# Counting longer landing times, and later TensorE requests, in the emission clock of a two-layer attention and SwiGLU kernel

## The chip, the cores and the metric

The kernel runs on one core of one Trainium2 chip. The metric is the device time of one execution in microseconds (us). Every device time quoted is a median of repeated runs. A profile shows one execution (before's is a further one, of 1567.82 us), and its span is 1 to 2 us shorter than its device time. TensorE is called PE, VectorE DVE, ScalarE ACT, GpSimd POOL, SyncE SP. "L656" is line 656 of the kernel.

## The reference

Two layers, each an attention block A and a SwiGLU block B with residuals, over 2048 tokens of width 1024 (abridged).

```python
def _A_ref(x, wqkv, wo):            # H = 32 heads of 32; W, dil = 8, 2
    qkv = ((x @ wqkv).reshape(B, S, 3, H, Dh)).transpose(2, 0, 3, 1, 4)
    q, k, v = qkv[0], qkv[1], qkv[2]
    idx = arange(S)[:, None] - (arange(W) * dil)[None, :]
    # gathered kg, vg: for each token its own and seven earlier tokens, two apart
    logits = einsum("bhsd,bhswd->bhsw", q, kg) * Dh ** -0.5      # -1e9 where idx < 0
    o = einsum("bhsw,bhswd->bhsd", softmax(logits), vg)
    return o.transpose(0, 2, 1, 3).reshape(B, S, D) @ wo

def _B_ref(x, w1, w3, w2):          # F = 3584
    return (silu(x @ w1) * (x @ w3)) @ w2

x = A_x
x = x + _A_ref(_layernorm(x), A_wqkv, A_wo)
x = x + _B_ref(_layernorm(x), B_w1, B_w3, B_w2)
x = x + _A_ref(_layernorm(x), A_wqkv, A_wo)        # the same weights again
x = x + _B_ref(_layernorm(x), B_w1, B_w3, B_w2)
```

## The kernel before

PE does the projections. The eight-neighbour attention has no matmul in its inner part: DVE multiplies q with shifted k (L582), folds the products (L502, L506), PE adds up heads with a 0/1 matrix (the "gather", L595), a softmax follows (DVE L616 to L628, ACT L620), POOL spreads the result over the partitions by four DMAs into `At` (L635), DVE multiplies `At` with shifted v and folds again (L656), and PE multiplies the result `oT` with wo (L762). One such round covers 256 tokens and is called a half here; there are 16.

Three stages follow each other. Stage A is layer 0's projections, up to the first gate matmul of B. The middle stage is the first two chunks of B (pg L1243, pu L1252, acc L1274). During it ACT and DVE also prepare scaled sums and differences of w1, w3 and w2 and store them to HBM. In the last stage the other six chunks of B use those stored sums with fewer matmuls (st L1122, w L1057). The rest of the attention is woven in everywhere.

All engines' instruction streams are written in an order that an *emission clock* decides while the program is built. `now["pe"]`, `now["dve"]`, `now["act"]` advance by counted costs. Background work is emitted when the clock says that it can run before the next thing which must be on time. At run time the engines take their streams in order and wait where data is missing, as the traces show it: in before DVE stood 5.96 us at one product with later instructions behind it, and PE 4.85 us at one matmul.

The parts of the kernel that matter here, cut where `...` stands:

```python
def background(until):                 # DVE work that fits before `until`
    while True:
        best = None
        for queue in (norms, makes, adds, values, scores):
            step = head(queue)
            if step is not None:
                start = max(now["dve"] + 0.3, step[1])
                if start - 0.3 + step[0] <= until and (best is None or start < best[0]):
                    best = start, queue
        if best is None:
            return
        take(best[1])

def pe_requests(limit=1, must=False):  # small matmuls that DVE or ACT asked PE for
    act_background()
    while pe_queue and limit and (must or pe_queue[0][0]() + 2.5 <= now["pe"]):
        pe_queue.pop(0)[1]()
        limit -= 1

def score_steps():                     # ... q, k products, gather, softmax, then
        At = Ats[l, h] = wk.tile([P, 4, W, BLK], BF16, name="At")
        for a in range(4):
            heads = An[32 * a:32 * (a + 1)]...
            nc.gpsimd.dma_start(At[:, a]..., heads)          # L635
        At_at[l, h] = now["dve"] + 6.0

def value_steps():
        ...
        yield 0.0, max(ready, At_at[l, h]), lambda: None     # not before At has landed
        yield from tree(KT, tree_bufs[1], mul_v, ...)        # L656: At * v

def weight_size(m, g, w, at, got):     # ACT sums squares of w1/w3, PE adds them up (L872)
        ...
        t = now["act"] + 0.3
        pe_queue.append((lambda: t, lambda: add_up(t)))      # the scaled copies wait for it
```

Of the kernel before, what the change touches and what calls it, by code (L numbers as in the profile page):

```python
# [17 lines left out]
def kernel(  # L18
# [67 lines left out]
    now = dict(pe=23.6, dve=15.0, act=24.5, table=None, sp=12.0, dma=31.5)  # L86
# [268 lines left out]
    def act_background():  # L355
        for queue in (acts, sizes, parts, reads):
            while True:
                s = head(queue)
                if s is None or max(now["act"], s[1]) + s[0] > now["pe"] + 2.2:
                    break  # L360
                take_act(queue)
# [180 lines left out]
    def load_qk(l, h):  # L542
        if (l, h) in qks or (l, h // R, 1) not in qkv_at:
            return
        qT = qkvp.tile([P, KT, TCH], BF16, name="qT")
        kT = qkvp.tile([P, KT, HALO + TCH], BF16, name="kT")
        load_part(qT, l, 0, h * TCH, False)
        qks[l, h] = qT, kT, load_part(kT, l, 1, h * TCH, True)
# [7 lines left out]
    pe_queue = []  # L556
    L_at, At_at, Ats, av_done = {}, {}, {}, set()
# [3 lines left out]
    def pe_requests(limit=1, must=False):  # L561

        act_background()
        while pe_queue and limit and (must or pe_queue[0][0]() + 2.5 <= now["pe"]):
            pe_queue.pop(0)[1]()
            limit -= 1

    def score_steps():

        V = nc.vector  # L570
        for g, (l, h) in enumerate(halves):
            load_qk(l, h)
            while (l, h) not in qks:
                yield "blocked"
                load_qk(l, h)
            load_v(l, h)
            qT, kT, ready = qks[l, h]
            psm = wk.tile([P, W, 2, TCH], BF16, name="psm")

            def mul_qk(w_, pr):  # L580
                k0 = HALO - DIL * w_
                V.tensor_tensor(pr, qT[:], kT[:, :, k0:k0 + TCH], op=ALU.mult)  # L582

            yield 0.0, ready, lambda: None
            yield from tree(W, tree_bufs[0], mul_qk, lambda w_: psm[:, w_], True)
            load_v(l, h)
            if g + 1 < len(halves):
                load_qk(*halves[g + 1])
            at = {}

            def gather_heads(t):
                at["L"] = L = side.tile([P, W, BLK], FP32, name="L", tag="sd")
                for i in range(2):
                    for a in range(4):
                        nc.tensor.matmul(L[32 * a:32 * (a + 1), :, :], lhsT=gather[:],  # L595
                                         rhs=psm[:, :, i, a * BLK:(a + 1) * BLK], start=i == 0, stop=i == 1,
                                         skip_group_check=True)
                at["t"] = pe(3, t) + 0.2

            while g and halves[g - 1] not in At_at:  # L600
                yield "blocked"
            t = now["dve"] + 0.2
            pe_queue.append((lambda: t, lambda: gather_heads(t)))
            while "t" not in at:
                yield "blocked"
            L = at["L"]
            mx = smp.tile([P, BLK], FP32, name="mx")
            E = smp.tile([P, W, BLK], BF16, name="E")
            sm_ = smp.tile([P, BLK], FP32, name="sm_")
            rs = smp.tile([P, BLK], FP32, name="rs")  # L610
            An = E
            yield 0.0, at["t"], lambda: None
            if h == 0:
                yield 0.2, 0.0, lambda: V.tensor_tensor(L[0:32, :, 0:HALO], L[0:32, :, 0:HALO], maskT[:],
                                                        op=ALU.add)
            yield 0.68, 0.0, lambda: V.tensor_reduce(mx[:], L[:].rearrange("p w e -> p e w"), op=ALU.max, axis=AX.X)  # L616

            def exps():
                V.tensor_tensor(L[:], L[:], mx[:].unsqueeze(1).to_broadcast([P, W, BLK]), op=ALU.subtract)
                nc.scalar.activation(E[:], L[:], ACTF.Exp, scale=scale)  # L620
                at["E"] = act(0.65, now["dve"] + 0.1, "exp")

            yield 0.70, 0.0, exps
            yield 0.0, at["E"] if "E" in at else 0.0, lambda: None
            yield 0.66, at["E"], lambda: V.tensor_reduce(sm_[:], E[:].rearrange("p w e -> p e w"), op=ALU.add,
                                                         axis=AX.X)
            yield 0.56, 0.0, lambda: V.reciprocal(rs[:], sm_[:])
            yield 0.68, 0.0, lambda: V.tensor_tensor(An[:], E[:], rs[:].unsqueeze(1).to_broadcast([P, W, BLK]),  # L628
                                                     op=ALU.mult)
            while g >= 1 and halves[g - 1] not in av_done:  # L630
                yield "blocked"
            At = Ats[l, h] = wk.tile([P, 4, W, BLK], BF16, name="At")
            for a in range(4):
                heads = An[32 * a:32 * (a + 1)].rearrange("h w e -> h (w e)").unsqueeze(1).to_broadcast([32, 4, W * BLK])
                nc.gpsimd.dma_start(At[:, a].rearrange("p w e -> p (w e)"), heads)  # L635
            At_at[l, h] = now["dve"] + 6.0

    def value_steps():

        V = nc.vector  # L640
        for g, (l, h) in enumerate(halves):
            while (l, h) not in At_at or (g >= 2 and o_todo.get(halves[g - 2], 1)):
                yield "blocked"
            load_v(l, h)
            while (l, h) not in vs:
                yield "blocked"
                load_v(l, h)
            At = Ats[l, h]
            vT, ready = vs[l, h]
            oT = wk.tile([P, KT, TCH], BF16, name="oT", bufs=2)  # L650
            oTs[l, h] = oT

            def mul_v(t, tm):
                base = vT[:, t, HALO:HALO + TCH]
                win = bass.AP(vT.tensor, base.offset, [list(base.ap[0]), [-DIL, W], [BLK, 4], [1, BLK]])
                V.tensor_tensor(tm.rearrange("p w (a e) -> p w a e", a=4), At[:].rearrange("p a w e -> p w a e"), win, op=ALU.mult)  # L656

            yield 0.0, max(ready, At_at[l, h]), lambda: None
            yield from tree(KT, tree_bufs[1], mul_v, lambda t: oT[:, t, :], False)
            oT_at[l, h] = now["dve"]  # L660
            o_todo[l, h] = 2
            av_done.add((l, h))
            if g + 1 < len(halves):
                load_v(*halves[g + 1])
# [189 lines left out]
    def weight_size(m, g, w, at, got):  # L854

        w_ = w[:].rearrange("p k c -> p (k c)")
        half = w_.shape[1] // 2
        up, down = up_scale[:, m, g:g + 1], down_scale[:, m, g:g + 1]
        for i in range(2):
            yield 1.95, at, lambda: nc.scalar.activation(junk, w_[:, i * half:(i + 1) * half], ACTF.Square,  # L860
                                                         accum_out=size[:, m, g, i:i + 1])

        def scale_item(ps, r):
            def emit():
                scale_of(ps[:], up, down)
                got["at"] = now["dve"] + 0.1
            yield 0.8, r, emit

        def add_up(t):
            ps = side.tile([P, 1], FP32, name="size", tag="sd")  # L870
            for i in range(2):
                nc.tensor.matmul(ps[:], lhsT=ones[:], rhs=size[:, m, g, i:i + 1], start=i == 0, stop=i == 1)  # L872
            makes.append([scale_item(ps, pe(2, t)), None])

        t = now["act"] + 0.3
        pe_queue.append((lambda: t, lambda: add_up(t)))

    def weight_sums(m, g, w, got):
# [78 lines left out]
    def scales2():  # L957

        def scale_item(ps, r):
            def emit():  # L960
                nc.vector.tensor_reduce(total[:], ps[:], op=ALU.add, axis=AX.X)
                scale_of(total[:], up2[:], down2[:])
                got2["at"] = now["dve"] + 0.1
            yield 1.1, r, emit

        def add_up(t):
            ps = side.tile([P, 16], FP32, name="size", tag="sd")
            nc.tensor.matmul(ps[:], lhsT=ones[:], rhs=size2[:], start=True, stop=True)
            makes.append([scale_item(ps, pe(1, t)), None])

        t = now["act"] + 0.3
        pe_queue.append((lambda: t, lambda: add_up(t)))

    got2 = {}
# [401 lines left out]
```

## Time and profile before

| | before |
|---|---|
| median of 3 runs (range) | 1570.33 us (1569.12 to 1570.57) |
| span of the profiled execution | 1566.1 us |
| PE stream at its own pace (below) | about 1519 us |
| PE waits, sum | 30.2 us |
| idle of DVE before value products L656 | 41.8 us |

The PE stream's own pace is a sum over its 9694 matmuls with the spacing that the trace shows when nothing is waited for (0.216 us between 128x512 matmuls, 0.109 between 128x256 ones). These are the head and two lines of the first part of the profile page:

```profile
span 1566.1 us, 25184 instructions
...
PE 1531.8 (98%) x9694; PEld 993.9 (63%) x9694; DVE 1193.6 (76%) x2048; ACT 881.6 (56%) x1386; POOL 155.0 (10%) x308
```

PE is busy 98% of the span, so only its gaps can be won. The next list, the waits of PE, says what each gap waited for: the waiting instruction and its line, what ended the wait, then total us, times, longest.

```profile
PE st L1122 <- DVE st L1163: 5.3, 2, 4.8
PE w L1057 <- DVE hsum L1028: 4.2, 3, 1.8
PE L L595 <- DVE psm L506: 3.9, 2, 2.7
PE w L1057 <- DVE hT L1028: 3.0, 4, 1.5
PE size L968 <- ACT hsum L937: 2.6, 1, 2.6
PE st L1122 <- ACT big L1160: 2.0, 1, 2.0
PE po L762 <- DVE x_sb L767: 1.7, 1, 1.7
PE w L1057 <- ACT big L1077: 1.7, 4, 0.6
PE pu L1252 <- DMA w3t<-in_B_w_dram: 1.4, 1, 1.4
PE st L1122 <- DVE big L1175: 1.4, 1, 1.4
PE po L762 <- DVE oT L506: 1.3, 2, 1.1
```

Left out are two start-up waits, 1.8 us together. No entry is larger than 5.3 us. Seven of the eleven, 20.8 of 28.5 us, name DVE, which is itself busy only 76% of the time, so DVE is not too slow but late at certain places. Its own waits show one that is plainly a scheduling matter:

```profile
DVE st L1163 <- ACT big L1160: 48.5, 27, 3.6
DVE tree L656 <- DMA At<-E: 38.1, 12, 7.3
...
DVE tree L656 <- DMA late<-t_d: 3.6, 1, 3.6
```

The value products wait 38.1 us for `At` in 12 of 16 halves (the 41.8 us of the table are these and the 3.6 us of the last line). How that reaches PE shows in the timeline around 860 us (start, duration, instruction, and in brackets the idle time before it with what ended it), first DVE, then PE:

```profile
852.00 1.55 DVE L1042 SCALAR_TENSOR_TENSOR x_sb<-w,down,x_sb 128x512 bf16<-128x512 f32 x2
859.51 1.23 DVE L656 TENSOR_TENSOR tree<-At,vT 128x2048 bf16<-128x2048 bf16 x1 [5.96 <-DMA At<-E]
...
862.98 0.69 DVE L1163 TENSOR_TENSOR st<-st,big 128x512 f32<-128x512 f32 x1
```

```profile
857.84 1.04 PE L1122 MATMUL st<-big,early 128*128 128x256 f16 x8
863.72 1.82 PE L1122 MATMUL st<-big,late 128*128 128x256 f16 x8 [4.85 <-DVE st L1163]
```

DVE stood 5.96 us at its value product. The addition L1163 that PE needed for its next block stood four instructions behind (at 862.98; the lines between are products and folds of the same half), and DVE did not pass over the waiting product in those 5.96 us. PE idled 4.85 us. The eight 128x256 matmuls that follow also took 1.82 us together instead of the usual 1.03 or so; the section on the result comes back to that.

### The profile page before, as it was taken

What the parts mean: (1) busy time and instruction counts of PE and PEld (TensorE: products, weight loads), DVE (VectorE), ACT (ScalarE), POOL (GpSimd) and SP (SyncE); (2) the same over time, 40 slices, a digit from 0 to 9 for tenths busy, and PEclk for the clock granted to TensorE, in tenths of its full rate; (3) what the DMA queues carried; (4) which work ended last, traced back from release to release, by engine and by line L of the source; (5) the groups of instructions that cost most, each with busy time, mean ns of one, the idle gap of its engine ahead of it and who ended that gap; (6) DMA issues with size and microseconds to landing.
All of it is one profiled execution on the core that took longest, in us unless ns stands there. A gap on an engine that the chain in (4) does not pass through costs nothing.

```text
span 1566.1 us, 25184 instructions
## 1 busy us (share of the span) xinstructions
PE 1531.8 (98%) x9694; PEld 993.9 (63%) x9694; DVE 1193.6 (76%) x2048; ACT 881.6 (56%) x1386; POOL 155.0 (10%) x308
## 2 busy tenths in 40 slices
PE   9999989999999999899999999999999999999999
PEld 7666634444444578575675757866677657676866
DVE  4789797888978879989796968897577977445345
ACT  3785366576566346555465554655648346544634
POOL 1210101111121100101011010100102000000000
PEclk9999999999999999999999999999999999999999
DMA  9676959699788898979979888897979977878885
GB/s 323 188 215 220 220 167 348 237 324 313 226 286 312 276 335 292 303 246 307 308 257 296 288 283 271 298 327 263 319 270 298 337 274 270 313 272 320 324 293 208
DMA packets 261432, 439.57 MB, mean 281 GB/s; under 512 B 73856, under 2 KB 201088, under 8 KB 245056
## 3 DMA queue, kind: packets, MB, share of 16 engines
q1 hardware_dynamic: 248464, 390.90, 75.2%
q0 software_dynamic: 12704, 46.93, 8.3%
q8 instruction: 76, 1.25, 0.3%
q14 instruction: 44, 0.36, 0.1%
q10 hardware_dynamic: 144, 0.13, 0.0%
HBM read 345.90 MB, written 67.90 MB: 264 GB/s over the span
## 4 chain that ended last, share of the span: by engine, by line
PE 77%; DVE 12%; DMA 7%; ACT 2%; issue 1%; POOL 1%; SPq 0%; DVEq 0%; ACTq 0%
PE st L1122 29%; PE ps L820 13%; PE w L1057 11%; PE po L762 6%; PE acc L1274 6%; PE pu L1252 5%; PE pg L1243 5%; DMA At<-E 3%; DVE tree L656 2%; DVE tree L502 2%; DVE tree L582 1%; DMA x_sb<-in_A_x_dram 1%; DMA w3t<-in_B_w_dram 1%; DVE hT L1028 1%; POOL At L635 1%
## 5 line engine op out<-in xcount | busy, mean ns | idle before, releaser
L820 PE MATMUL ps<-xnT,wqkv 128*128 128x512 f16 (+1 forms) x1472 | 320.7, 379 | 0.0
L1122 PEld LDWEIGHTS <-early 128*128 128x128 f16 x2688 | 263.3, 98 | 38.5 <-issue 1.0
L820 PEld LDWEIGHTS <-wqkv 128*128 128x128 bf16 x1472 | 210.7, 144 | 108.5 <-issue 2.5
L1057 PE MATMUL w<-t,hT 128*128 128x512 f16 x1008 | 226.5, 379 | 4.8 <-DVE hT L1028 3.0
L1122 PEld LDWEIGHTS <-late 128*128 128x128 f16 x2016 | 197.3, 98 | 40.1 <-issue 11.9
L656 DVE TENSOR_TENSOR tree<-At,vT 128x2048 bf16<-128x2048 bf16 x128 | 156.2, 1220 | 43.2 <-DMA At<-E 38.1
L1122 PE MATMUL st<-xnT,late 128*128 128x256 f16 x1344 | 174.3, 273 | 3.5 <-ACT big L1160 2.0
L582 DVE TENSOR_TENSOR tree<-qT,kT 128x2048 bf16<-128x2048 bf16 x128 | 156.3, 1221 | 26.5 <-DMA qT<-qkv_d 15.8
L502 DVE TENSOR_TENSOR tree<-tree 128x1024 bf16<-128x1024 bf16 x256 | 175.1, 684 | 0.9
L1057 PEld LDWEIGHTS <-hT 128*128 128x128 f16 x1008 | 98.0, 98 | 118.8 <-DVE hT L1028 5.8
L1122 PE MATMUL st<-big,early 128*128 128x256 f16 x1344 | 173.1, 273 | 0.3
L1122 PE MATMUL st<-xnT,early 128*128 128x256 f16 x1344 | 165.7, 273 | 0.0
L1151 ACT COPY st<-st 128x512 f32<-128x512 f32 x84 | 48.4, 576 | 127.3 <-PE st L1122 126.5
L762 PE MATMUL po<-wo,oT 128*128 128x512 bf16 x512 | 116.2, 379 | 3.0 <-DVE x_sb L767 1.7
L1252 PE MATMUL pu<-xnT,w3t 128*128 128x512 f16 x448 | 105.8, 379 | 1.4 <-DMA w3t<-in_B_w_dram 1.4
L1243 PE MATMUL pg<-xnT,w1t 128*128 128x512 f16 x448 | 107.1, 382 | 0.0
L824 ACT CAST hT<-ps 128x512 bf16<-128x512 f32 x96 | 55.7, 585 | 81.9 <-PE ps L820 78.4
L1274 PE MATMUL acc<-w2t,hT 128*128 128x512 bf16 x448 | 98.2, 379 | 0.0
L1163 DVE TENSOR_TENSOR st<-st,big 128x512 f32<-128x512 f32 x84 | 58.4, 695 | 48.7 <-ACT big L1160 48.5
L1131 ACT ACTIVATE sg<-st,down_scale 128x512 bf16<-128x512 f32 x126 | 86.4, 686 | 12.3 <-PE st L1122 11.8
L1122 PE MATMUL st<-big,late 128*128 128x256 f16 x672 | 87.9, 274 | 5.3 <-DVE st L1163 5.3
L762 PEld LDWEIGHTS <-oT 128*128 128x128 bf16 x512 | 50.0, 98 | 59.3 <-DVE oT L506 2.1
(166 smaller groups left out, 1905.9 us busy)
## 6 DMA issues: line engine op xcount, KB each, us to landing
early<-t_d SPq DMA_DIRECT2D x84, 1024.0 KB, 6.7
late<-t_d SPq DMA_DIRECT2D x84, 768.0 KB, 6.3
t<-t_d SPq DMA_DIRECT2D x42, 1024.0 KB, 6.8
t<-t_d SPq DMA_DIRECT2D x42, 768.0 KB, 5.3
wqkv<-in_A_wqkv_dram SPq DMA_DIRECT2D x28, 1024.0 KB, 8.5
w1t<-in_B_w_dram SPq DMA_DIRECT2D x14, 1024.0 KB, 8.4
w3t<-in_B_w_dram SPq DMA_DIRECT2D x14, 1024.0 KB, 11.8
t_d<-big POOLq DMA_DIRECT2D x28, 512.0 KB, 6.6
```

What stands on the lines that cost most here:

```text
L502: nc.vector.tensor_tensor(b, b, buf[:, 4:8, :], op=ALU.add)
L582: V.tensor_tensor(pr, qT[:], kT[:, :, k0:k0 + TCH], op=ALU.mult)
L656: V.tensor_tensor(tm.rearrange("p w (a e) -> p w a e", a=4), At[:].rearrange("p a w e -> p w a e"), win, op=ALU.mult)
L762: nc.tensor.matmul(ps[:], lhsT=oT[:, t, j * P:(j + 1) * P], rhs=wo[:, t, hh * 512:(hh + 1) * 512], start=(t == 0), stop=(t == KT - 1))
L820: nc.tensor.matmul(ps[:], lhsT=ws[kk // KH][:, kk % KH, t::KT], rhs=xnT[:, kk, :], start=(kk == 0), stop=(kk == KT - 1))
L1057: nc.tensor.matmul(out[:], lhsT=lhs[:, k, j * P:(j + 1) * P], rhs=w[:, k, :], start=start and k == 0, stop=k == nq - 1, skip_group_check=True)
L1122: nc.tensor.matmul(out[:, a, :], lhsT=w[:, a, blk, k, :], rhs=rhs[:, k, :], start=start and a == 0 and k == 0, stop=k == KQ - 1, skip_grou ...
L1131: nc.scalar.activation(sg[:], src, ACTF.Silu, scale=inv)
L1163: nc.vector.tensor_tensor(G["D"][:], G["D"][:], su, op=ALU.add)
L1243: nc.tensor.matmul(pg[:], lhsT=w1t[:, kk, fi * P:(fi + 1) * P], rhs=xnT[:, kk, :], start=(kk == 0), stop=(kk == KT - 1))
L1252: nc.tensor.matmul(pu[:], lhsT=w3t[:, kk, fi * P:(fi + 1) * P], rhs=xnT[:, kk, :], start=(kk == 0), stop=(kk == KT - 1))
L1274: nc.tensor.matmul(acc[:], lhsT=hT[:, f, j * P:(j + 1) * P], rhs=tiles[hh][f // nq][:, f % nq, :], start=(f == 0), stop=(f == f1 - f0 - 1))
```

## The change

The intent is that the emission clock should believe in longer latencies: `At` lands 11 us after its issue and not 6; q, k, v loads land 2 us later; small matmuls asked from PE stand 1 us later in its stream, and those for weight scales 2.2 us more. No arithmetic is added or removed. In before the 64 `At` pieces of 128 KB took 2.7 to 12.0 us from issue to landing, median 6.3; from the end of the product L628 to the last of a half's four landings it was 5.1 to 13.3 us.

```diff
@@ pe_requests
-        while pe_queue and limit and (must or pe_queue[0][0]() + 2.5 <= now["pe"]):
+        while pe_queue and limit and (must or pe_queue[0][0]() + 3.5 <= now["pe"]):
@@ score_steps
-            yield 0.0, ready, lambda: None
+            yield 0.0, ready + 2.0, lambda: None
...
-            At_at[l, h] = now["dve"] + 6.0
+            At_at[l, h] = now["dve"] + 11.0
@@ value_steps
-            yield 0.0, max(ready, At_at[l, h]), lambda: None
+            yield 0.0, max(ready + 2.0, At_at[l, h]), lambda: None
@@ weight_size, and the same line in scales2 (w2)
-        t = now["act"] + 0.3
+        t = now["act"] + 2.5
```

More of the change, by code (lines that the diff above doesn't have):

```diff
@@ L969, in add_up @@
             makes.append([scale_item(ps, pe(1, t)), None])
-        t = now["act"] + 0.3
+        t = now["act"] + 2.5
         pe_queue.append((lambda: t, lambda: add_up(t)))
```

## The prediction

> **What bounds it now.** TensorE. The page gives PE 98% busy (1531.8 of 1566.1 us), VectorE 76%, ScalarE 56%, clock 0.998. A 128x512 matmul issues every 0.216 us: about 1519 us for the PE stream. The waits of PE add up to only 30 us: st on VectorE's L1163 5.3, w on hsum 4.2 and on hT 3.0, the gather L on psm 3.9, size (L968) on hsum 2.6, st on ACT L1160 2.0, po on x_sb 1.7 and on oT 1.3, w on ACT L1077 1.7, pu on the w3t load 1.4, st on L1175 1.4, start-up 1.8. So about 28 us (1.8%) is the ceiling of what a reordering can give.
>
> **What the change does.** It adds and removes no arithmetic. The clock only decides where instructions stand in each in-order stream. [...]DVE waited 5.96 us for At before its tree at 859.5, the addition L1163 behind it came late, and PE sat 4.85 us.
>
> 1. At counted 11 us after its issue instead of 6. From the end of the E product (L628) to the last At piece's landing takes 5.1 to 13.3 us, median 8.8: 6 was nearly always too short. VectorE waited 38.1 us for At in 12 of 16 halves. In the new order the VectorE work between that product and the first value product, summed with measured durations, grows from typically 6 to 8 us to 11 to 12 (up to 18; one half keeps none). The waits for At should fall from 38 to under 12 us.
> 2. q, k and v counted 2 us later: small; the 15.8 us wait for the first qT is a start-up matter and stays.
> 3. PE requests 1 us later, weight-scale requests 2.2 us more: the first two gathers (stalls 2.7 and 1.2) and the size matmul (2.6) stand 16 matmuls, 3.4 us, later. Those 6.5 us should go. The fifth o tile, stalled 2.7 us around 207 to 220, stands 14 us later.
>
> ACT gets two more table loads, 1.28 us each.
>
> **Sum.** Late requests: -6. PE stalls behind At waits (L1163, hsum, hT, L1175, L1160, po: 18.6 us in all): perhaps two thirds, -12. New collisions in the reshuffled stream: +3. Net -15 us: 1555 us, range 1547 to 1564. Faster by over 2% needs 31 us, more than all stalls: 0.02. Slower by 2%: 0.01.
>
> **What the profile would show if right.** VectorE's waits for At under 12 us; waits of PE near 15 us in total, with the gather and the size matmul gone from the list; the 4.85 us stall near 860 gone; PE and VectorE busy times equal (1532, 1194 us). If At waits fall but PE waits stay near 30, new collisions ate the gain; if At waits stay, landing times grew, because DMAs moved too.
>
> **What would make it wrong.** Delayed value trees delay oT, the o tiles, the norm and its transposes: if one of those becomes what PE waits for at the start of a B stage, some us are lost each time (no such wait is there today). A softmax pushed onto a spot where ScalarE must switch tables just before the gate's silu (as near 626) can stall PE 2 to 5 us. Shifted loads can collide: late weights, like the w3t near 475, would show as PE waiting for a DMA.

On table loads, the traces show 27 in before and 29 in after, 1.28 us each, and near 626 us in before a PE wait of 2.01 us behind two of them; the 5 us of "2 to 5 us" is not shown.

## The result

| | before | after |
|---|---|---|
| median (range), 4 runs each | 1569.72 us (1565.77 to 1570.57) | 1546.71 us (1546.08 to 1548.26) |
| profiled span | 1566.1 us | 1546.5 us |
| PE waits, sum | 30.2 us | 12.5 us |
| idle of DVE before L656 | 41.8 us | 6.5 us |

The ratio is 0.986 (95% interval 0.9841 to 0.9879). Ratios here are the mean time of one kernel's runs over that of the other's of the same rounds, so not quite the ratio of the medians. The interval is far from 1: the change is worth about 22 us, or 1.4%.

The head of the page after, to set beside the one of before:

```profile
span 1546.5 us, 25176 instructions
...
PE 1529.9 (99%) x9694; PEld 992.7 (64%) x9694; DVE 1191.9 (77%) x2048; ACT 883.3 (57%) x1388; POOL 158.8 (10%) x308
```

Busy times of PE, DVE and ACT are the same within 2 us: only the gaps shrank. The waits of PE after:

```profile
PE L L595 <- DVE psm L506: 4.1, 1, 4.1
PE w L1057 <- DVE hT L1028: 2.6, 3, 1.4
PE w L1057 <- ACT big L1077: 1.9, 4, 0.6
...
PE po L762 <- DVE x_sb L767: 0.9, 1, 0.9
...
PE st L1122 <- DVE big L1178: 0.7, 1, 0.7
```

The waits on L1163, hsum, x_sb, oT, L1160, w3t and the size matmul (L968) are gone or below 1 us; the lines left out are of start-up or under 0.3 us. There is one new wait above 1 us: a gather waited 4.1 us for psm, near 546 us. And DVE's waits for `At`:

```profile
DVE tree L656 <- DMA At<-E: 6.5, 2, 5.3
```

The stall near 860 us has become this. The half is the same, and DVE now reaches its value product with other work done:

```profile
841.17 1.22 DVE L582 TENSOR_TENSOR tree<-qT,kT 128x2048 bf16<-128x2048 bf16 x1
...
844.50 0.69 DVE L1163 TENSOR_TENSOR st<-st,big 128x512 f32<-128x512 f32 x1
846.35 1.23 DVE L656 TENSOR_TENSOR tree<-At,vT 128x2048 bf16<-128x2048 bf16 x1 [1.16 <-DMA At<-E]
```

From the end of the product L628 to the last landing, `At` took 11.9 us in this half (12.8 in before). DVE now waits 1.16 us instead of 5.96, and the addition L1163 stands in front of the value product.

**Half speed after a stall.** The trace records the granted PE clock. Two windows of before (the stall near 860 us and the 3.5 us after it), then two of after (the gather's stall and the 5.8 us after it); the columns are length, PE busy and instructions, granted clock, DMA share, GB/s:

```profile
858.80:863.70 4.90, 0.08 (x1) 1.00 1.04 402
863.70:867.20 3.50, 3.48 (x17) 0.51 0.58 232
```

```profile
542.10:546.10 4.00, 0.00 (x0) 0.88 1.06 352
546.10:551.90 5.80, 5.74 (x20) 0.50 1.06 366
```

The half clock is recorded for 3.41 us each at 198.2 and 863.8 us in before and for 6.83 us at 545.2 us in after, and in it 128x256 matmuls came 0.213 us apart instead of 0.109, 128x512 ones 0.427 instead of 0.216. In after it began 1.0 us before the stall ended. As an estimate from these lengths and the granted half, each stretch loses at most another 1.7 us in before and 3.4 in after. Start-up and tail left out, these two traces hold five PE gaps of 2.0 us or more: half clock came with those of 4.85 and 2.59 us (before, near 864 and 198 us) and 4.06 us (after), and not with those of 2.67 and 2.01 us (before, near 63 and 629 us). The length of the stall alone does not tell the two kinds apart here, and what does is not shown. So these three stalls cost more than their own length.

**Where the time went, by stage.** Stage A ends at PE's first gate matmul (L1243), the middle stage at its first L1122. One profile each; the experiments below are in the table for reference. DVE's first product (L582), which waits for the first q load, starts anywhere from 43.3 us (at_only, at_8) to 45.2 us (before, size_only), so up to 1.9 us of a difference in stage A is start-up, not order.

| kernel | stage A | middle | last | span | PE waits A / middle / last | idle before L656 |
|---|---|---|---|---|---|---|
| before | 199.0 | 373.2 | 993.9 | 1566.1 | 8.3 / 4.4 / 17.4 | 41.8 |
| after | 191.6 | 375.2 | 979.7 | 1546.5 | 1.9 / 5.0 / 5.6 | 6.5 |
| at_only | 192.9 | 382.2 | 976.2 | 1551.3 | 2.8 / 12.2 / 3.8 | 7.6 |
| requests_only | 191.4 | 400.0 | 999.1 | 1590.5 | 1.7 / 21.9 / 20.1 | 33.2 |
| size_only | 195.4 | 382.0 | 998.2 | 1575.6 | 5.4 / 13.0 / 18.9 | 39.2 |
| limit_only | 192.3 | 393.7 | 999.6 | 1585.5 | 2.3 / 20.7 / 19.2 | 40.5 |
| loads_only | 195.5 | 374.7 | 995.4 | 1565.6 | 5.6 / 7.2 / 17.1 | 40.8 |
| at_and_requests | 192.4 | 373.3 | 983.5 | 1549.2 | 2.5 / 4.7 / 7.7 | 12.1 |
| wo_for_at | 197.2 | 370.8 | 976.6 | 1544.6 | 6.6 / 3.6 / 3.8 | 4.8 |
| requests_wo | 192.1 | 398.3 | 979.5 | 1569.9 | 3.0 / 22.6 / 5.0 | 4.4 |
| at_8 | 191.2 | 393.0 | 987.2 | 1571.4 | 1.6 / 20.5 / 12.0 | 13.1 |
| at_13 | 191.7 | 394.6 | 981.2 | 1567.4 | 1.9 / 18.4 / 7.6 | 5.2 |
| at_16 | 195.5 | 374.9 | 977.6 | 1548.0 | 3.8 / 6.1 / 4.8 | 9.4 |
| after_turned_3 | 191.2 | 368.0 | 981.2 | 1540.4 | 2.2 / 0.9 / 6.8 | 8.7 |

The change won 7.4 us in stage A and 14.2 us in the last stage, and lost 2.0 us in the middle one.

### The profile page after: what moved, and what is told of

It reads as the page before. It is cut to its first block, busy times and chain, and to the rows that moved or that the text cites. A ratio compares the mean times of both kernels' runs of the same rounds, so it can differ in the third digit from the quotient of the medians.

```text
span 1546.5 us, 25176 instructions
## 1 busy us (share of the span) xinstructions
PE 1529.9 (99%) x9694; PEld 992.7 (64%) x9694; DVE 1191.9 (77%) x2048; ACT 883.3 (57%) x1388; POOL 158.8 (10%) x308
## 4 chain that ended last, share of the span: by engine, by line
PE 83%; DVE 9%; ACT 3%; DMA 3%; issue 1%; POOL 1%; SPq 1%; ACTq 0%; DVEq 0%; POOLq 0%
PE st L1122 28%; PE ps L820 18%; PE w L1057 11%; PE po L762 7%; PE pg L1243 6%; PE acc L1274 6%; PE pu L1252 6%; DVE tree L656 1%; DMA wqkv<-in_A_wqkv_dram 1%; DVE tree L502 1%; PE pq L436 1%; DVE tree L582 1%; DVE hT L1028 1%; DMA xnT<-xn 1%; DVE hT L1140 1%
## 5 line engine op out<-in xcount | busy, mean ns | idle before, releaser
L1122 PEld LDWEIGHTS <-early 128*128 128x128 f16 x2688 | 262.8, 98 | 38.2 <-issue 1.4
L1122 PEld LDWEIGHTS <-late 128*128 128x128 f16 x2016 | 197.0, 98 | 31.2 <-issue 3.2
L582 DVE TENSOR_TENSOR tree<-qT,kT 128x2048 bf16<-128x2048 bf16 x128 | 156.3, 1221 | 30.0 <-ACT big L824 14.8
L1122 PE MATMUL st<-xnT,late 128*128 128x256 f16 x1344 | 174.2, 273 | 1.0 <-DVE big L1178 0.7
L1122 PE MATMUL st<-big,early 128*128 128x256 f16 x1344 | 172.2, 273 | 0.2
L1122 PE MATMUL st<-xnT,early 128*128 128x256 f16 x1344 | 165.7, 273 | 0.0
L656 DVE TENSOR_TENSOR tree<-At,vT 128x2048 bf16<-128x2048 bf16 x128 | 156.2, 1220 | 7.9 <-DMA At<-E 6.5
L1243 PE MATMUL pg<-xnT,w1t 128*128 128x512 f16 x448 | 105.8, 379 | 0.0
L1163 DVE TENSOR_TENSOR st<-st,big 128x512 f32<-128x512 f32 x84 | 58.4, 695 | 51.9 <-ACT big L1160 51.8
L1122 PE MATMUL st<-big,late 128*128 128x256 f16 x672 | 87.1, 273 | 0.0
```

Of the source, the lines that this page charges most:

```text
L582: V.tensor_tensor(pr, qT[:], kT[:, :, k0:k0 + TCH], op=ALU.mult)
L656: V.tensor_tensor(tm.rearrange("p w (a e) -> p w a e", a=4), At[:].rearrange("p a w e -> p w a e"), win, op=ALU.mult)
L1122: nc.tensor.matmul(out[:, a, :], lhsT=w[:, a, blk, k, :], rhs=rhs[:, k, :], start=start and a == 0 and k == 0, stop=k == KQ - 1, skip_grou ...
L1163: nc.vector.tensor_tensor(G["D"][:], G["D"][:], su, op=ALU.add)
L1243: nc.tensor.matmul(pg[:], lhsT=w1t[:, kk, fi * P:(fi + 1) * P], rhs=xnT[:, kk, :], start=(kk == 0), stop=(kk == KT - 1))
```

## The experiments

Twelve kernels ran, in three calls. Each was compared with runs of before on the same chip, in five rounds. Before's medians were 1568.71, 1567.22 and 1568.85 us. All results were correct except where a wrong one was made on purpose.

| run | median us (range) | ratio to before (95%) |
|---|---|---|
| at_only | 1556.26 (1553.03 to 1557.0) | 0.9923 (0.991 to 0.9936) |
| requests_only | 1590.81 (1587.99 to 1593.07) | 1.0142 (1.0127 to 1.0156) |
| loads_only | 1568.96 (1566.81 to 1570.93) | 1.0003 (0.9992 to 1.0015) |
| wo_for_at | 1547.82 (1545.51 to 1549.54) | 0.9868 (0.9854 to 0.9881) |
| size_only | 1581.76 (1577.33 to 1583.31) | 1.0082 (1.0063 to 1.0102) |
| limit_only | 1587.12 (1585.32 to 1592.63) | 1.0129 (1.0109 to 1.015) |
| at_and_requests | 1550.33 (1549.05 to 1550.98) | 0.9887 (0.9869 to 0.9905) |
| at_8 | 1574.99 (1573.14 to 1578.35) | 1.005 (1.003 to 1.007) |
| requests_wo | 1571.58 (1568.7 to 1574.3) | 1.0019 (1.0 to 1.0037) |
| at_13 | 1565.77 (1565.21 to 1569.18) | 0.9986 (0.9968 to 1.0003) |
| at_16 | 1547.74 (1545.93 to 1549.72) | 0.9864 (0.9845 to 0.9883) |
| after_turned_3 | 1543.39 (1542.23 to 1545.51) | 0.9841 (0.982 to 0.9861) |

### First call: the parts alone

**at_only**

```diff
-            At_at[l, h] = now["dve"] + 6.0
+            At_at[l, h] = now["dve"] + 11.0
```

> Only At counted 11 us after its issue. Theory (VectorE's waits for At hold up work that TensorE needs; they are the larger part of the gain): VectorE's waits for At fall from 38 to under 12 us, and the time falls by 11 to 17 us against before; the gather and size stalls (6.5 us) stay. Rival 1 (TensorE's own requests stood too early, and that is the gain): less than 8 us. Rival 2 (any reshuffle gives a few us, no single wait matters): between 0 and 8 us, whatever the waits for At do.

12 us faster, inside the theory's range. Idle before L656 fell from 41.8 to 7.6 us. The expectation that the gather and size stalls would stay was wrong: the gathers' 3.9 us shrank to 0.8 and the size matmul no longer waited. At the first gather (2.7 to 0.8 us) this is not the change's doing: PE's and DVE's orders are the same up to there, but DVE's first product started at 43.33 us instead of 45.15. Why the second gather and the size matmul no longer waited was not traced. The middle stage got 9.0 us longer (waits for w3t, 5.8 us, which before had only 1.4).

**requests_only**

```diff
-  ... pe_queue[0][0]() + 2.5 <= now["pe"]
+  ... pe_queue[0][0]() + 3.5 <= now["pe"]
-        t = now["act"] + 0.3        # in both places
+        t = now["act"] + 2.5
```

> Only the later TensorE requests (3.5 and 2.5). Theory: the two gather stalls (3.9 us) and the size stall (2.6 us) go from the waits of PE, VectorE's waits for At stay near 38 us, time 4 to 8 us under before. Rival 1 (requests are most of the gain): 12 us or more under before.

A plain miss for the theory and for its rival: 22 us *slower*. The gather and size stalls did go (stage A: 191.4 us, 7.6 less than before), but the middle stage grew by 26.8 us. Its waits of PE:

```profile
PE pu L1252 <- DMA w3t<-in_B_w_dram: 7.0, 2, 3.6
PE ps L820 <- ACT hT L824: 6.9, 1, 6.9
...
PE acc L1274 <- DVE hT L1256: 3.7, 2, 2.3
```

The 6.9 us wait for ACT's hT stands at 544 to 551 us, 40 us before the middle stage ends. The chain of waits behind it is a serial one (start, length, what), with ACT's scaled copies of w2 waiting (18.5 us in two waits) for the store that frees their staging buffer:

```profile
530.17 9.19 DMA t_d<-big
...
539.38 4.16 ACT big L984 x7
543.54 4.34 DMA t_d<-big
...
548.61 1.93 ACT big L984 x3
...
551.06 5.09 PE ps L820 x12
```

So the weight preparation, which needs the scale requests first, ended up late, and PE waited for the ACT instruction behind it in ACT's stream.

**loads_only**

```diff
-            yield 0.0, ready, lambda: None
+            yield 0.0, ready + 2.0, lambda: None
-            yield 0.0, max(ready, At_at[l, h]), lambda: None
+            yield 0.0, max(ready + 2.0, At_at[l, h]), lambda: None
```

> Only q, k and v counted 2 us later. Theory: nothing, within 3 us of before, waits for At still 30 us or more. Rival 2 (any reshuffle gives a few us): 3 to 10 us faster.

Nothing, as the theory said: ratio 1.0003, idle before L656 40.8 us.

**wo_for_at**, before's own order without the wait (wrong result)

```diff
-            At = Ats[l, h]
+            At = Ats[l, h] if g < 2 else wo[:, 0:2, :]...   # resident, same shape and type
```

> The kernel before in its own order, but from the third half on the value products read two rows of the resident wo instead of At, so there is no landing to wait for; wrong result on purpose. At is still written by the same DMAs. Theory: waits for At of 33 us (all but the first two halves) go, the PE stalls on L1163, hsum, hT, L1175 and po shrink, time 10 to 17 us under before with no order changed. Rival 2 (order, not the wait, makes the time): under 4 us.

21 us faster, a little more than expected (the ratio times before's 1568.7 is 1548.0), with every instruction of PE, DVE and ACT in the same place and the same DMAs issued. This is the direct price of waiting for `At` in before: idle before L656 falls to 4.8 us (the first two halves), and the waits of PE to:

```profile
PE pu L1252 <- DMA w3t<-in_B_w_dram: 2.8, 1, 2.8
PE L L595 <- DVE psm L506: 2.7, 2, 1.8
PE st L1122 <- ACT big L1160: 2.0, 1, 2.0
PE size L968 <- ACT hsum L937: 2.0, 1, 2.0
```

L1163, hsum and L1175 are gone. The gather and size stalls (still 2.7 and 2.0 us; the first two halves still wait for `At` here) and those on w3t and L1160 stay. The rival that only the order matters is out: here the order did not change.

### Second call: the parts of the requests, and the dose

**size_only**

```diff
-        t = now["act"] + 0.3        # in both places
+        t = now["act"] + 2.5
```

> Only the two weight-scale requests counted 2.2 us later (0.3 to 2.5). In the built order all gathers but two stand where they stood in before, the w2 size matmul stands 3.4 us later. Theory A (a request placed later only removes its own stall): the 2.6 us size stall goes, everything else stays, 1 to 4 us under before. Theory B (later scale requests delay the scales, the scaled copies and the release of w1 and w3, and this made the requests-only kernel slow): 10 us or more over before, with waits of PE for w3t or for ACT's hT.

13 us slower by the ratio: theory A is wrong. The size stall went, but in the profile, which is of the fastest of its six runs (4.4 us under their median), the middle stage is 8.8 us longer and the last 4.3. Theory B does not get its signs either (w3t 1.2 us, no wait for ACT's hT): PE waited instead for x_sb (6.8 us in 4 waits), hT and st from DVE.

**limit_only**

```diff
-  ... pe_queue[0][0]() + 2.5 <= now["pe"]
+  ... pe_queue[0][0]() + 3.5 <= now["pe"]
```

> Only the limit of all TensorE requests, 2.5 to 3.5. In the built order the gathers 4 to 14 come 7 to 39 us later than in before, as in the requests-only kernel; the last size matmul at 476 instead of 486 us of stream. Theory C (the later limit pushes the softmax of each half into a later, more crowded place, and the delays add up): 8 to 22 us over before, gather and size stalls gone, At waits about 30 us, new PE stalls of st, hT and hsum. Theory B says near before or a little faster.

19.9 us slower on the medians, as theory C said, with the same long wait for ACT's hT (6.2 us) though the last size matmul stood where theory B would have it harmless. The idle time before L656 was 40.5 us, not the 30 that it named, and the more crowded place of the softmax that it gives as the cause is not shown.

**at_and_requests**, the change without the load part

> The change without the load part. If the loads part matters nothing also in company, 1545 to 1551 us and waits for At under 12 us. If the order as a whole is a matter of luck, anywhere between 1545 and 1570.

1550.33 us, inside the first range; idle before L656 was 12.1 us, just over the bound. The load part may be worth the 3.6 us that separate the medians, but the two were not on the same chip, the ratios' intervals overlap, and alone it was worth nothing.

**at_8**, the whole change with another number

```diff
-            At_at[l, h] = now["dve"] + 11.0     # as in after
+            At_at[l, h] = now["dve"] + 8.0
```

> The whole change, but At counted 8 us, not 11. Landing takes 5 to 13 us, median near 9. In the built order its gathers 4 to 14 follow the late track of the requests-only kernel, and the last size matmul stands at 486 us of the stream. Theory (the longer the count up to the true landing, the better, smoothly): 1552 to 1560 us. Theory C (the track decides, At above 10 keeps it from being late): 1568 to 1592 us, with a PE wait of about 7 us for ACT's hT near 545 and At waits of 10 to 25 us.

1574.99 us: *slower than before*, with a 7.2 us wait of PE for ACT's hT and 13.1 us idle before L656. The smooth theory is out.

### Third call: two separate causes

**requests_wo**, requests_only in its own order, without the wait for At (wrong result)

> The requests-only kernel (1591 us, 22 over before) in its own order, but from the third half on the value products read rows of the resident wo instead of At: no wait for At. Wrong result on purpose. Theory I (late requests hurt only because VectorE, held by At, runs behind the clock, so the weight scales and their stores come late): 1545 to 1560 us, the 6.9 us wait of PE for ACT's hT near 544 at most 2 us. Theory J (late scale requests hurt by themselves, through the chain of scaled copies and stores): 1570 us or more, that wait still over 4 us.

Of the two, J's numbers came: the loss does not need the wait for `At`. That the *scale* requests make it, as J says, is not shown: size_only, which delays these alone, has no such wait for ACT's hT, and limit_only, which delays all requests by 1 us, has it (6.2 us). Taking the wait away is worth 19 us here too (1590.81 to 1571.58), nearly what it is worth in before's order (21), and all of it in the last stage (999.1 to 979.5). The middle stage stays at 398.3 us with the same waits:

```profile
PE ps L820 <- ACT hT L824: 7.3, 1, 7.3
PE pu L1252 <- DMA w3t<-in_B_w_dram: 7.0, 2, 3.9
PE acc L1274 <- DVE hT L1256: 3.7, 2, 2.3
```

So two effects are nearly independent: the wait for `At`, and a place-dependent loss in the middle stage.

**at_13**

```diff
-            At_at[l, h] = now["dve"] + 11.0     # as in after
+            At_at[l, h] = now["dve"] + 13.0
```

> The whole change with At counted 13 us. Its gathers 7 to 14 follow the late track of the 8 us kernel (1575 us), but the count covers every landing seen but one. Theory I (At covered: VectorE keeps to the clock): 1545 to 1556 us, waits for At under 8 us. Theory C (the track decides): 1565 us or more.

1565.77 us, so theory I by itself fails, and theory C's bound is met. The waits for `At` are gone all the same (5.2 us, all of it in the one half that has no other work in this order), and the last stage is 981.2 us, as good as after's. The middle stage is 394.6 us.

**at_16**

```diff
-            At_at[l, h] = now["dve"] + 11.0     # as in after
+            At_at[l, h] = now["dve"] + 16.0
```

> The whole change with At counted 16 us, more than any landing seen (13.3). Theory I: no less good than 11, 1543 to 1554 us, waits for At under 3 us (the half that has no other work keeps its 5 us). If counting too long costs (idle VectorE, late o tiles), 1556 us or more.

1547.74 us, level with after: counting more than any landing seen costs nothing by itself. The middle stage is 374.9 us here. One half, the one that has no other work in this order, waits 9.4 us for its `At`, the other fifteen not at all, so "under 3 us" held for those and "its 5 us" did not.

**after_turned_3**, the whole change plus one more latency

```diff
-            turned.append(dma(420, max(now["dve"], free), 1.3))          # and the same line for ACT
+            turned.append(dma(420, max(now["dve"], free), 1.3) + 3.0)
```

> The whole change and the transposes of the norm counted 3 us longer to their landing. After has a new PE wait of 4.1 us near 542 for a gather, whose psm stands behind four sums that wait 10 us for transposes; 11 matmuls at half speed follow it (2.4 us). If the count moves those sums behind psm, both go: 1538 to 1543 us, better than after. If the sums stay in front, 1545 to 1550 us.

1543.39 us, the fastest kernel, though just outside the 1538 to 1543 us expected if both go, and both went. In after, DVE stood 10.08 us for transposes with the last psm folds behind them, and the gather's PE stall came from there. The two transposes, issued by SP one after the other from 531.30 us, took 5.4 and 3.3 us to issue and landed 9.9 and 5.3 us after the start of their issue; the emission clock counted 1.3 us for each issue. First after, then this kernel:

```profile
530.91 1.23 DVE L582 TENSOR_TENSOR tree<-qT,kT 128x2048 bf16<-128x2048 bf16 x1
542.21 0.69 DVE L287 TENSOR_TENSOR big<-xnT 128x1024 f16<-128x1024 f16 x1 [10.08 <-DMA xnT<-xn]
...
545.68 0.42 DVE L506 TENSOR_TENSOR psm<-tree 128x512 bf16<-128x512 bf16 x1
```

```profile
535.39 0.68 DVE L502 TENSOR_TENSOR tree<-tree 128x1024 bf16<-128x1024 bf16 x1
536.11 0.43 DVE L506 TENSOR_TENSOR psm<-tree 128x512 bf16<-128x512 bf16 x1
539.40 0.69 DVE L287 TENSOR_TENSOR big<-xnT 128x1024 f16<-128x1024 f16 x1 [2.87 <-DMA xnT<-xn]
```

```profile
543.05 0.62 PE L595 MATMUL L<-psm,gather 128*32 128x512 bf16 x8
543.59 15.77 PE L820 MATMUL ps<-xnT,wqkv 128*128 128x512 f16 x72
```

The sums L287 now stand behind the last psm, and the gather L595 has no idle time before it. The middle stage fell from 375.2 to 368.0 us, with 0.9 us of PE waits, and no half-speed stretch is left between the start-up and the tail: the granted clock of the profiled execution is recorded as 1.0, where one stretch of 3.41 us would leave 0.999. The step from after is about 3 us. The runs' ranges do not touch (1542.23 to 1545.51 against 1546.08 to 1548.26), but they come from different calls.

### The clock against the chip

The emission clock can be read out when the program is built; no chip is needed for it (gathers are compared at their ends). Its own end of the PE stream hardly differs between these kernels. The chip's last matmul does:

| kernel | clock's end | chip's last matmul starts | chip minus clock at the end | at the 6th gather | at the 7th gather |
|---|---|---|---|---|---|
| before | 1529.8 | 1562.2 | 32.4 | 11.2 | 12.5 |
| after | 1528.3 | 1542.6 | 14.3 | 0.2 | 4.8 |
| at_only | 1527.9 | 1547.4 | 19.5 | 15.5 | 15.4 |
| requests_only | 1530.5 | 1586.2 | 55.7 | 15.2 | 32.4 |
| at_8 | 1530.3 | 1567.4 | 37.1 | 9.6 | 25.2 |
| at_13 | 1529.2 | 1563.5 | 34.3 | 7.9 | 26.6 |
| at_16 | 1527.5 | 1544.1 | 16.6 | 8.6 | 10.7 |
| after_turned_3 | 1534.2 | 1536.1 | 1.9 | -0.2 | -0.5 |

A comparison of the clock's end would have ranked these eight wrongly: it calls the best of them the slowest. What it does show is where chip and clock part. In after they agree within 1 us up to the sixth gather; in after_turned_3 within 4 us at every gather. In requests_only, at_8 and at_13 the chip loses 16 to 19 us between the sixth and the seventh gather, where the weight preparation ends.

## Why the prediction was right or wrong

**What bounds the kernel, and the ceiling: right, slightly low.** PE was the bound and only its gaps shrank: its waits fell by 17.7 us in the profiles, whose spans differ by 19.6. The ceiling of 28 us left out the half-speed stretches after stalls, which in before lasted 6.8 us and, as an estimate from the granted half, cost up to 3.4 us.

**At: right in mechanism, too small in size.** The waits for `At` fell from 38.1 to 6.5 us (predicted: under 12). That the wait was the cause is shown by wo_for_at, where it was removed without moving an instruction. I had booked two thirds of the 18.6 us of PE stalls behind it, 12 us. Of those entries (L1163, hsum, hT, L1175, L1160, po; they add up to 18.9) 3.7 us remain in after, so 15 us came back. In wo_for_at 3.1 us remain, 2.0 of them L1160's, which therefore did not come from `At`. The step that was mis-sized is "perhaps two thirds, -12".

**Later requests: right about the stalls they stand for, wrong as a term of the sum.** "Those 6.5 us should go" came true in stage A: 7.6 us shorter with that part alone, of which up to 1.8 us is the earlier first product (43.39 for 45.15 us). But the term "-6" supposed that a request placed later costs nothing elsewhere, and that is the step that failed. Alone it made the kernel 22 us slower, through waits for w3t, ACT's hT and DVE's hT in the middle stage (requests_only, and requests_wo without any wait for At). It also was not needed for those stalls: at_only shortened stage A by 6.1 us. The two parts fix the same stalls there and do not add up.

**Loads: right alone** (1.0003); in company, at most a few us, not settled.

**New collisions, +3: about right in number, wrong in kind.** One appeared, a 4.1 us gather wait with 5.8 us at half speed behind it. I had feared table loads, late weights, and late transposes of the norm at the start of a B stage. It did come from such transposes, whose issue took 5.4 and 3.3 us where the clock counted 1.3, but by another path: DVE's sums waited for them, and the folds that the gather needed stood behind. Counting 3 us more for the transposes removed it.

**Signs named beforehand.** Total PE waits near 15: measured 12.5. Size matmul gone from the list: yes. Gather gone: the two old ones yes, a new one came. The 4.85 us stall near 860 gone: yes. Busy times equal: PE 1529.9 for 1532, DVE 1191.9 for 1194.

**The total** was 15 us predicted and 22 us measured (1555 against 1546.71, a hair under the range's lower end of 1547; before's median times the ratio gives 1547.7). In the profiled pair, whose spans differ by 19.6 us, the waits account for 17.7: the entries booked under `At` gave 15.2 (12 booked), the old gather and size waits 6.5 (6 booked), w3t 1.4 (none booked), against 4.1 of the new gather wait (3 booked) and 1.3 us of small ones. So the At term, small by 3 us, is the largest miss. Half speed explains nothing of this pair: 6.8 us of it are recorded in each of the two traces. Over all runs it may explain some: the granted clock was 0.993 to 0.999, mean 0.9964, in the 33 runs of before beside the experiments, and 0.997 to 1.0, mean 0.9983, in after's four, which as an estimate (span times the missing share) is about 3 us. The request term did not spoil it because together with the At part an order came out whose middle stage is short (375.2 us, and 373.3 without the load part); nothing in my argument foresaw that.

**What stays open.** In some of the built orders the middle stage takes 368 to 375 us and in others 382 to 400. The side does not follow from the size of a number: At at 11 and 16 falls on the short side, 8 and 13 on the long one. What PE waits for there is shown (w3t, ACT's hT behind the scaled copies, DVE's hT, and x_sb in size_only and at_only); which decision of the emitter sends an order to the bad side is not. There is a mark that can be read before a run: the "late track" of the gathers in the built order, named beforehand, put at_8 and at_13 on the bad side rightly. But size_only has a long middle stage (382.0 us) without it, so it is a mark and not the cause. A candidate is the counted landing of the weight stores: 7 us from DVE's last difference, where the trace of after shows a median of about 8.4 us for w1 and w3 and 9.5 for w2. Counting 8 to 10 us there made the emission clock's own end 15 to 100 us later, so those versions were built but not run, and the candidate is only argued.

## What to carry to other kernels

In this order, fixed ahead of time, `At` was counted at 6 us where it landed 5.1 to 13.3 us after its producer's end, and DVE waited 38.1 us for it with needed work behind; so measure each landing from its producer's end and count at least what is seen. For the value products themselves too long was cheaper here than too short (idle before L656 5.2 and 9.4 us at 13 and 16, 13.1 us at 8), but the whole kernel at 13 was 19 us slower than at 11, through the middle stage. Judge each such number by a run and by stage: a dial can win 12.7 us in one stage and lose 21.4 in another (at_13 against before), and neighbouring settings (8, 11, 13, 16) need not lie on a curve. To price a wait, replace what is waited for by something resident in the same order; and compare the chip's time with the clock's at fixed marks to find where they part.
